# Seven block products for eight in the gate and value layers of the last two token tiles

## The chip, the cores and the metric

The program runs on one core of a Trainium2 chip. The metric is the time of the whole program in device microseconds. Beside the plain runs, one execution was profiled; its trace has a time, a unit and a source line for every instruction. The units are named as in the profile: PE does the matmuls, PEld loads their weights, DVE and ACT work element by element and read PE's results out of PSUM, POOL works element by element in SBUF, and SP issues the DMAs.

## What is computed

An attention with random features is followed by a gated feed-forward layer, all in float32:

```
proj = x @ omega.T                       # q and k, 8 batches, 8 heads, 576 rows, 64 -> 128 features
phi  = exp(proj - |x|^2/2 - max) / sqrt(128)
kv, z = phi(k).T @ v, sum(phi(k))        # per batch and head
attn  = (phi(q) @ kv) / (phi(q) @ z + 1e-6)
X     = attn, heads side by side         # 4608 tokens x 512
g, val = X @ w_gate, X @ w_val           # 512 -> 1536
out   = (silu(g) * val) @ w_out          # 1536 -> 512
```

## The kernel before, in words

**Tiles and operands.** The tokens lie in nine tiles of 512, numbered 0 to 8. The 1536 columns of the hidden layer are twelve blocks `f` of 128, in four sets of three. For the feed-forward layer every float32 operand is held as two parts, `hi` (rounded by ACT) and `lo` (the remainder, subtracted by POOL or DVE), and a product is three matmuls: hi·hi, hi·lo, lo·hi. `x` is kept as `xh`, `xl` in four rotating buffers, weights as `whi`, `wlo`.

**A visit** is one tile with one set of blocks. `stream` issues it: for each of the three blocks a gate product `g` (`mm1`, L633 to L641: four chunks of 128 along 512, three matmuls each, so 12 matmuls of 128x512 into one PSUM bank), SiLU on ACT (L707), then a value product `v` (12 matmuls), the product with the gate on DVE (L721), the hi part of the result `hh` on ACT (L724) and its lo part `hl` on POOL (L725). Four down products `o` of 9 matmuls each follow (`down`, `mm2`, L644 to L650), one for each 128 tokens. They are put into a float32 accumulator `acc`: for the first set by a copy on ACT (L671), after that by an addition on DVE (L674); after the last set the rows are stored (L678). A visit is 3·12 + 3·12 + 4·9 = 108 matmuls. When the next visit uses another set, its weights are loaded into three rotating buffers `wraw` from a scratch array in HBM, rounded by ACT (L242) and subtracted by POOL (L243).

**Rounds.** `ROUNDS` (L60) says which tiles go through the four sets together: 0 to 2, 3 and 4, 5 and 6, 7 and 8.

**Attention** runs in 72 steps of two groups of 256 rows. A step projects on PE (`st_project`, `pp`, L393), takes maxima on DVE, exponentials on ACT (L425), and so on, down to `q_out`, which puts the finished rows into `xh`, `xl` (L626, L627). Attention has four PSUM banks (pools `ps_p`, `ps_a`, `ps_k`) and the SBUF pool `att`; the feed-forward layer has the other four banks (`ps_m`).

**What sets the order.** `course` (L182 to L199) is a plan: for each attention step, how much of the stream of visits shall have been issued by then. It is a string pulled tight between a lower bound (a buffer of `x` must come free) and an upper bound (a tile must be complete), and it ends at the last step at `upper[NN]` (L192). The main loop issues, at six places in a step, as much of the stream as the plan is owed; after the loop whatever is left follows. A scheduler then orders the instructions of each engine; each engine executes its own in order.

Of the kernel before, what the change touches and what calls it, by code (L numbers as in the profile page):

```python
# [23 lines left out]
def kernel(  # L24
# [34 lines left out]

    ROUNDS = [range(0, 3), range(3, 5), range(5, 7), range(7, 9)]  # L60

# [20 lines left out]
    ps_m = ctx.enter_context(tc.tile_pool(name="ps_m", bufs=4, space=PSUM))  # L82
    att = ctx.enter_context(tc.tile_pool(name="att", bufs=2))
    ps_p = ctx.enter_context(tc.tile_pool(name="ps_p", bufs=2, space=PSUM))
    ps_a = ctx.enter_context(tc.tile_pool(name="ps_a", bufs=1, space=PSUM))
    ps_k = ctx.enter_context(tc.tile_pool(name="ps_k", bufs=1, space=PSUM))

# [103 lines left out]
    course = (lower + upper) / 2  # L191
    course[0], course[NN] = 0.0, upper[NN]  # L192
    for _ in range(20000):
# [40 lines left out]

    def new_weights(f, i):
        hi = wpool.tile([P, DM], F32R, name=f"whi{f}_{i}", tag=f"whi{i}")
        lo = wpool.tile([P, DM], F32R, name=f"wlo{f}_{i}", tag=f"wlo{i}")
        weights[f, i] = hi, lo
# [50 lines left out]

    def load_weights(f, i):  # L290
        need(f, i)
        new_weights(f, i)
        raw = moe.tile([P, DM], F32, name=f"wraw{f}_{i}", tag="wraw", bufs=3)
        nc.sync.dma_start(raw, wscr[f, i])
        split_piece(f, i, raw)
# [367 lines left out]
    def down(j, k_, ht, wts, next_set, tt):  # L663
        fs = sorted(ht)
        po = ps_moe(f"o{j}_{k_}_{tt}", [P, DM])
        for n, f in enumerate(fs):
            need(f, 2)
            mm2(po, ht[f], weights[f, 2] if wts is None else wts[f], tt, n == 0, n == FA - 1)
        if k_ == 0:
            acc[j, tt] = accp.tile([P, DM], F32, name=f"acc{j}_{tt}", tag="acc")  # L670
            nc.scalar.copy(acc[j, tt], po)  # L671
        else:
            a_ = acc[j, tt]
            nc.vector.tensor_tensor(a_, po, a_, op=ALU.add)  # L674
        if k_ == NSET - 1:
            a_ = acc.pop((j, tt))
            for o in range(0, P, RES):
                nc.sync.dma_start(rows_of(TILES[j][0] + tt * P + o), a_[o : o + RES, :])  # L678
        if next_set is not None and tt == TILES[j][1] // P - 1:
            for n in range(FA):  # L680
                load_weights(next_set * FA + n, 2)

    def stream():

        todo = []
        for vi, (j, s_, k_) in enumerate(visits):
            nxt = visits[vi + 1] if vi + 1 < len(visits) else None
            new_set = nxt and nxt[1] != s_
            w = TILES[j][1]
            while not avail(j):  # L690
# [18 lines left out]
            if new_set:  # L709
                for f in fs:  # L710
                    load_weights(nxt[1] * FA + f - fs[0], 0)
            while todo:
                down(*todo.pop(0))
                yield MM2
            for f in fs:
# [11 lines left out]
                if new_set:  # L727
                    load_weights(nxt[1] * FA + f - fs[0], 1)
            at_visit[0] = vi + 1
            wts = {f: weights[f, 2] for f in fs} if vi else None  # L730
            todo = [(j, k_, ht, wts, nxt[1] if new_set else None, tt) for tt in range(w // P)]
        for a in todo:
            down(*a)
            yield MM2
# [63 lines left out]
    for n in range(NN):  # L798
# [5 lines left out]
        for what in order:  # L804
            if what is not SHARE:
                what(n)
            if n < EARLY or what is SHARE:
# [5 lines left out]
                left -= 1  # L813
        load_z(n)
    for _ in ma:
        pass
# [30 lines left out]
```

## Time and profile before

| | us |
|---|---|
| median of 3 runs | 1244.59 |
| lowest, highest | 1243.67, 1246.83 |
| the profiled execution | 1241.44 |
| its span, first to last instruction | 1239.3 |
| PE busy in the span | 1206.6 |
| ACT, DVE, POOL busy | 585.3, 520.7, 504.4 |

In the answers of the trace, a group's row gives line, engine, operation, output and inputs by the program's names, shapes, count, then busy time and the mean of one in ns, then the idle time before them and what ended it. A window's row gives, for each engine, busy us and in brackets the instructions, then the granted clock of PE as a share of full speed, the busy share of the DMA engines and GB/s. A row of the chain of work that ended last gives start, length, engine, tile, line, count.

### The profile page before, as it was taken

Reading aid. Unit: us, or ns where it says so; the run is one execution under the profiler, and the core shown is the slowest. Engines: PE = TensorE matmul, PEld = TensorE weight load, DVE = VectorE, ACT = ScalarE, POOL = GpSimd, SP = SyncE. Lnnn points to the kernel's source line nnn. Section 1 sums busy time; section 2 is a strip of 40 time slices with the busy share of each in tenths; the row PEclk is TensorE's granted clock in tenths of the full one; section 3 lists DMA queues with packets and bytes.
Section 4 is the critical chain, followed back from the end, with each engine's and each line's share of the span. In section 5 each row is a group of like instructions: output and inputs, shape, how many; then the busy total and the mean of one; then the engine's idle time right before and its main releaser. Section 6 shows DMA issues by size and latency. Waiting matters only on the chain. (4 is left out here: it accounts for less than half of the span.)

```text
span 1239.3 us, 18373 instructions
## 1 busy us (share of the span) xinstructions
PE 1206.6 (97%) x6849; PEld 991.8 (80%) x6849; DVE 520.7 (42%) x1068; ACT 585.3 (47%) x1310; POOL 504.4 (41%) x436
## 2 busy tenths in 40 slices
PE   6999998999999999999999999989999999999998
PEld 5888787788888888877888878867887877788886
DVE  4887867435556424443334444332233322002212
ACT  3878775543445334455654465434634422332220
POOL 3333334354534322335554453335645421333431
PEclk7999999999999999999999999999999999999999
DMA  5555545324334322222222222212201021111202
GB/s 147 140 139 150 147 139 149 109 76 136 108 94 139 85 62 54 63 71 77 69 60 71 58 64 60 52 35 61 69 26 51 27 60 34 51 51 30 61 13 69
DMA packets 157689, 97.76 MB, mean 79 GB/s; under 512 B 119680, under 2 KB 132000, under 8 KB 157600
## 3 DMA queue, kind: packets, MB, share of 16 engines
q1 hardware_dynamic: 157600, 96.59, 29.3%
q8 instruction: 54, 0.88, 0.3%
q14 instruction: 35, 0.29, 0.1%
HBM read 77.66 MB, written 18.89 MB: 78 GB/s over the span
## 5 line engine op out<-in xcount | busy, mean ns | idle before, releaser
L243 POOL TENSOR_TENSOR wlo<-wraw,whi 128x512 fp32r<-128x512 f32 x108 | 139.1, 1298 | 157.9 <-ACT whi L242 157.7
L725 POOL TENSOR_TENSOR hl<-sl,hh 128x512 fp32r<-128x512 f32 x108 | 140.3, 1302 | 121.3 <-ACT hh L724 121.2
L650 PE MATMUL o<-whi,hh 128*128 128x512 f32 x432 | 172.9, 401 | 2.0 <-ACT hh L724 2.0
L425 ACT ACTIVATE ph<-pp,st 128x128 f32<-128x128 f32 x576 | 158.6, 382 | 32.8 <-DVE st L414 32.3
L650 PE MATMUL o<-whi,hl 128*128 128x512 f32 x432 | 169.6, 393 | 2.6 <-POOL hl L725 2.5
L641 PE MATMUL v<-xh,whi 128*128 128x512 f32 x432 | 172.0, 398 | 0.0
L641 PE MATMUL g<-xh,whi 128*128 128x512 f32 x432 | 171.0, 397 | 0.5 <-ACT xh L626 0.5
L641 PE MATMUL g<-xl,whi 128*128 128x512 f32 x432 | 169.0, 392 | 0.5 <-DVE xl L627 0.5
L650 PE MATMUL o<-wlo,hh 128*128 128x512 f32 x432 | 169.0, 391 | 0.0
L641 PE MATMUL v<-xl,whi 128*128 128x512 f32 x432 | 168.9, 391 | 0.0
L641 PE MATMUL v<-xh,wlo 128*128 128x512 f32 x432 | 168.8, 391 | 0.0
L641 PE MATMUL g<-xh,wlo 128*128 128x512 f32 x432 | 168.7, 391 | 0.0
L377 POOL TENSOR_TENSOR sq<-nat 128x512 f32<-128x512 f32 x72 | 76.6, 1065 | 186.7 <-DMA nat<-in_k_dram 135.4
L724 ACT CAST hh<-sl 128x512 fp32r<-128x512 f32 x108 | 67.1, 625 | 173.1 <-DVE sl L721 173.0
L674 DVE TENSOR_TENSOR acc<-o,acc 128x512 f32<-128x512 f32 x108 | 74.0, 688 | 170.6 <-PE o L650 170.4
L721 DVE TENSOR_TENSOR sl<-v,sl 128x512 f32<-128x512 f32 x108 | 74.0, 688 | 159.0 <-PE v L641 156.7
L242 ACT CAST whi<-wraw 128x512 fp32r<-128x512 f32 x108 | 66.8, 623 | 148.0 <-PE v L641 81.4
L411 DVE TENSOR_REDUCE st<-pp 128x4 f32<-128x512 f32 x144 | 93.5, 684 | 80.2 <-PE pp L393 79.9
L393 PE MATMUL pp<-omT,x 64*128 64x128 f32 x1152 | 97.8, 295 | 2.8 <-DVE xl L627 1.4
L393 PEld LDWEIGHTS pp<-omT,x 64*128 64x128 f32 x1152 | 80.7, 195 | 23.2 <-issue 14.6
L650 PEld LDWEIGHTS o<-whi,hh 128*128 128x128 f32 x432 | 81.6, 189 | 21.8 <-ACT hh L724 3.1
L650 PEld LDWEIGHTS o<-whi,hl 128*128 128x128 f32 x432 | 81.4, 189 | 21.7 <-POOL hl L725 4.3
(67 smaller groups left out, 1815.7 us busy)
## 6 DMA issues: line engine op xcount, KB each, us to landing
wraw<-wscr SPq DMA_DIRECT2D x108, 256.0 KB, 2.7
wscr<-wc SPq DMA_DIRECT2D x36, 256.0 KB, 2.3
out_dram<-acc SPq DMA_DIRECT2D x72, 128.0 KB, 2.4
nat<-in_k_dram SPq DMA_DIRECT2D x64, 128.0 KB, 3.1
v<-in_v_dram SPq DMA_DIRECT2D x64, 128.0 KB, 3.2
nat<-in_q_dram SPq DMA_DIRECT2D x64, 128.0 KB, 2.6
st<-in_moe_w_gate_dram SPq DMA_DIRECT2D x12, 512.0 KB, 5.3
st<-in_moe_w_val_dram SPq DMA_DIRECT2D x12, 512.0 KB, 4.1
```

What stands on the lines that cost most here:

```text
L242: nc.scalar.copy(hi, raw)
L243: nc.gpsimd.tensor_tensor(lo, raw, hi.bitcast(F32), op=ALU.subtract)
L377: nc.gpsimd.tensor_tensor(sq, nat, nat, op=ALU.mult)
L393: nc.tensor.matmul(pp[hh][:, i, c, :], x[r, i, c * P : (c + 1) * P], omT[r], start=True, stop=True)
L411: nc.vector.tensor_reduce(st[:, 1, :, :, hh], pp[hh], axis=AX.X, op=ALU.max, negate=True)
L425: nc.scalar.activation(ph[:, c, hh * M : (hh + 1) * M], pp[hh][:, i, c, :], AF.Exp, bias=st[:, 3, i, c, hh : hh + 1], scale=1.0,)
L641: nc.tensor.matmul(ps, a_[:, ws], b_[:, c, :], start=n == 0, stop=n == 3 * NC - 1)
L650: nc.tensor.matmul(ps, a_[:, ts_], b_, start=first and n == 0, stop=last and n == 2)
L674: nc.vector.tensor_tensor(a_, po, a_, op=ALU.add)
L721: nc.vector.tensor_tensor(h, pv, h, op=ALU.mult)
L724: nc.scalar.copy(hh, h)
L725: nc.gpsimd.tensor_tensor(hl, h, hh.bitcast(F32), op=ALU.subtract)
```

## The change

The last two tiles, 7 and 8, leave the rounds. Their gate and value products are done at the end, together, in six pairs of blocks (`pf` 0 to 5; each has a gate half, `i` = 0, and a value half, `i` = 1). For a pair, the weights are a 2x2 array of parts (two halves of the 512 inputs, two blocks), and `x` is another (two halves, two tiles). The four results are formed by seven products of parts, in Winograd's form, in place of eight: `a11·b11`, `a12·b21`, `s4·b22`, `a22·t4`, `s1·t1`, `s2·t2`, `s3·t3`, where the `s` are sums and differences of weight parts and the `t` of `x` parts. A product is two chunks by three matmuls, 6 matmuls of 128x512. Three PSUM banks `a`, `c`, `d` take the seven products of a half: `a` takes products 1, 6, 7, 4 on top of each other, `c` takes 5 and 3, `d` takes 2. What a bank holds in between is copied out by ACT (`m1`, `m5`, `u2`) and added on DVE (`plus`).

Around that:

- `load_seven` loads the two raw gate (or value) blocks of a pair, forms `s1` to `s4` on DVE (four operations of 128x256), rounds on ACT and subtracts on POOL. `make_t` forms the four `t` for all of `x`, two chunks with 8 DVE operations, 4 ACT roundings and 4 DVE subtractions of 128x512 each.
- Down products take two blocks (6 matmuls) for each 128 tokens, and the accumulator of tiles 7 and 8 gets six parts in place of four. The four `down` of tile 8 and then the four of tile 7 stand between the products of the next pair.
- When the attention loop is over, the pool `att` and the four PSUM banks of attention are closed, and the pools `win` (SBUF) and `ps_w` (four banks) take their place.
- The plan ends 25 us of stream (`MARGIN`) short of the end of its rounds.

The diff, cut to its core:

```
-    ROUNDS = [range(0, 3), range(3, 5), range(5, 7), range(7, 9)]
+    ROUNDS = [range(0, 3), range(3, 5), range(5, 7)]
+    LASTA, LASTB = 7, 8
+    NPF = NF // 2
+    MARGIN = 25.0
...
-    course[0], course[NN] = 0.0, upper[NN]
+    course[0], course[NN] = 0.0, upper[NN] - MARGIN
...
+    def load_seven(pf, i):
+        win = late_pools["win"]
+        raws_ = []
+        for f in (2 * pf, 2 * pf + 1):
+            raw = moe.tile([P, DM], F32, name=f"wraw{f}_{i}s", tag="wraw", bufs=3)
+            nc.sync.dma_start(raw, wscr[f, i])
+            raws_.append(raw)
+        (a11, a12), (a21, a22) = ((r[:, 0:G], r[:, G:DM]) for r in raws_)
+        s = win.tile([P, 4, G], F32, name=f"s{pf}_{i}", tag="s")
+        s1, s2, s3, s4 = (s[:, n] for n in range(4))
+        nc.vector.tensor_tensor(s1, a21, a22, op=ALU.add)
+        nc.vector.tensor_tensor(s3, a11, a21, op=ALU.subtract)
+        nc.vector.tensor_tensor(s2, s1, a11, op=ALU.subtract)
+        nc.vector.tensor_tensor(s4, a12, s2, op=ALU.subtract)
...
+            nc.scalar.copy(hi, src_)
+            nc.gpsimd.tensor_tensor(lo, src_, hi.bitcast(F32), op=ALU.subtract)
...
+    PROD = {1: ("a11", "b11"), 2: ("a12", "b21"), 3: ("s4", "b22"), 4: ("a22", "t4"), 5: ("s1", "t1"), 6: ("s2", "t2"), 7: ("s3", "t3")}
+    def product(ps, n, wts, start):
+        (wh, wl), (xh, xl) = wts[PROD[n][0]], ts[PROD[n][1]]
+        for c in range(CH):
+            w_ = slice(c * P, (c + 1) * P)
+            for m, (a_, b_) in enumerate(((wh, xh), (wh, xl), (wl, xh))):
+                nc.tensor.matmul(
+                    ps, a_[:, w_], b_[:, c, :],
+                    start=start and c == 0 and m == 0, stop=c == CH - 1 and m == 2, skip_group_check=True,
+                )
...
+            def gate(n, src_):
+                nc.scalar.activation(sl[n], src_, AF.Silu)
+            def value(n, src_):
+                nc.vector.tensor_tensor(sl[n], src_, sl[n], op=ALU.mult)
+                nc.scalar.copy(hh[:, n], sl[n])
+                nc.gpsimd.tensor_tensor(hl[:, n], sl[n], hh[:, n].bitcast(F32), op=ALU.subtract)
...
+                a, c, d = (ps_w.tile([P, T], F32, name=f"{e}{pf}_{i}", tag="w") for e in "acd")
+                product(a, 1, wts, True)
+                copy("m1", a)
+                product(c, 5, wts, True)
+                copy("m5", c)
+                if one_down():
+                    yield MM2
+                product(a, 6, wts, False)
+                copy("u2", a)
+                product(c, 3, wts, False)
+                plus(1, c, "u2")
+                if one_down():
+                    yield MM2
+                product(a, 7, wts, False)
+                plus(3, a, "m5")
+                product(d, 2, wts, True)
+                plus(0, d, "m1")
+                if one_down():
+                    yield MM2
+                product(a, 4, wts, False)
+                use(2, a)
+                if pf + 1 < NPF:
+                    load_seven(pf + 1, i)
+                if one_down():
+                    yield MM2
...
+    late.close()
...
+    late_pools["mt"] = make_t()
+    for _ in late_pools["mt"]:
+        give(1.0)
```

How the change moves instructions is shown at three places. **The first** is PE where attention step 67 begins (`g` and `v` are gate and value products of a visit, `pp` the projection of attention, `ptq` transposes). Before, the end of a value product and the next visit's gate:

```order
L641 MATMUL v_2_8496<-xh_6752,whi_1_7332 128x512
L641 MATMUL v_2_8496<-xl_6753,whi_1_7332 128x512
L641 MATMUL v_2_8496<-xh_6752,wlo_1_7333 128x512
L641 MATMUL g_3_8520<-xh_6028,whi_0_8430 128x512
L641 MATMUL g_3_8520<-xl_6029,whi_0_8430 128x512
L641 MATMUL g_3_8520<-xh_6028,wlo_0_8431 128x512
```

The same place now:

```order
L647 MATMUL v_2_8496<-xh_6752,whi_1_7332 128x512
L647 MATMUL v_2_8496<-xl_6753,whi_1_7332 128x512
L647 MATMUL v_2_8496<-xh_6752,wlo_1_7333 128x512
L399 MATMUL pp_67_8512<-omT,x_8373 128x128
L399 MATMUL pp_67_8513<-omT,x_8373 128x128
```

Up to this place PE's instructions are the same, one by one, in both programs (3588 of them). From here on a step has fewer matmuls of the stream: before, each of the steps 66 to 70 has 108 of them up to the next step's projection, now 72, 63, 69, 60 and 60. Behind the last attention matmul there were 756 and are now 999.

**The second** is ACT at the end of the first pair: `m_1` and `u_1` are copies out of the banks `c` and `a` of its value half, `whi_1_…` roundings of the next pair's value weights, `whi_2_…` of its down weights, `hh0s` the hi part of the result, `m_0` the first copy of the next pair. Before, ACT at the last change of a set of weights:

```order
L707 ACTIVATE sl_0_11035<-g_0_10996 128x512
L707 ACTIVATE sl_1_11037<-g_1_11009 128x512
L707 ACTIVATE sl_2_11039<-g_2_11022 128x512
L242 CAST whi_2_11085<-wraw_2_11087 128x512
L242 CAST whi_2_11091<-wraw_2_11093 128x512
L242 CAST whi_2_11097<-wraw_2_11099 128x512
L724 CAST hh_0_11117<-sl_0_11035 128x512
```

Now:

```order
L873 COPY u_1_10266<-a_1_10241 128x512
L248 CAST whi_2_10335<-wraw_2_10337 128x512
L783 CAST whi_1_1_10323<-s_1_10314 128x512
L861 CAST hh0s<-sl_1_10091 128x512
L248 CAST whi_2_10341<-wraw_2_10343 128x512
L783 CAST whi_1_2_10327<-s_1_10314 128x512
L861 CAST hh0s<-sl_3_10093 128x512
L783 CAST whi_1_3_10331<-wraw_1s 128x256
L861 CAST hh0s<-sl_0_10090 128x512
L861 CAST hh0s<-sl_2_10092 128x512
L873 COPY m_0_10362<-a_0_10353 128x512
```

Roundings that wait for a load now stand ahead of copies that PE waits for. **The third** is POOL at the same place, where it makes the lo parts. Before:

```order
L243 TENSOR_TENSOR wlo_2_10746<-wraw_2_10747,whi_2_10745 128x512
L243 TENSOR_TENSOR wlo_2_10752<-wraw_2_10753,whi_2_10751 128x512
L243 TENSOR_TENSOR wlo_2_10758<-wraw_2_10759,whi_2_10757 128x512
L725 TENSOR_TENSOR hl_3_10778<-sl_3_10695,hh_3_10777 128x512
L725 TENSOR_TENSOR hl_4_10796<-sl_4_10697,hh_4_10795 128x512
L725 TENSOR_TENSOR hl_5_10814<-sl_5_10699,hh_5_10813 128x512
```

Now:

```order
L784 TENSOR_TENSOR wlo_1_0_10320<-wraw_1s,whi_1_0_10319 128x512
L249 TENSOR_TENSOR wlo_2_10336<-wraw_2_10337,whi_2_10335 128x512
L784 TENSOR_TENSOR wlo_1_1_10324<-s_1_10314,whi_1_1_10323 128x512
L862 TENSOR_TENSOR hl0s<-sl_1_10091,hh0s 128x512
L249 TENSOR_TENSOR wlo_2_10342<-wraw_2_10343,whi_2_10341 128x512
L784 TENSOR_TENSOR wlo_1_2_10328<-s_1_10314,whi_1_2_10327 128x512
L862 TENSOR_TENSOR hl0s<-sl_3_10093,hh0s 128x512
```

The lo parts of the result (`hl0s`) stand among those of the next weights, where before they stood behind them.

More of the change, by code (lines that the diff above doesn't have):

```diff
@@ L233, with new_weights @@
     converted = set()
-    def new_weights(f, i):
-        hi = wpool.tile([P, DM], F32R, name=f"whi{f}_{i}", tag=f"whi{i}")
-        lo = wpool.tile([P, DM], F32R, name=f"wlo{f}_{i}", tag=f"wlo{i}")
+    def new_weights(f, i, pool=None):
+        hi, lo = (
+            (pool or wpool).tile([P, DM], F32R, name=f"w{e}{f}_{i}", tag=f"w{e}{i}") for e in ("hi", "lo")
+        )
         weights[f, i] = hi, lo
@@ L814 @@
         load_z(n)
+    late.close()
+    for name, pool in (
+        ("win", tc.tile_pool(name="win", bufs=1)),
+        ("ps_w", tc.tile_pool(name="ps_w", bufs=4, space=PSUM)),
+    ):
+        late_pools[name] = ctx.enter_context(pool)
+    late_pools["mt"] = make_t()
+    for _ in late_pools["mt"]:
+        give(1.0)
     for _ in ma:
```

124 lines of the change are left out of this document (111 added, 13 removed).

## The prediction, on record before the change was run

> **What bounds the kernel now.** I read the totals first, then windows, then the chain of waits from the end, then what PE waited for.
>
> ```profile
> span 1239.3 us, 18373 instructions
> PE 1206.6 (97%) x6849; PEld 991.8 (80%) x6849; DVE 520.7 (42%) x1068; ACT 585.3 (47%) x1310; POOL 504.4 (41%) x436
> ```
>
> PE is the only engine near the span. A share of 97% is an average, so the windows have to say where it holds:
>
> ```profile
> 620.00:744.00 124.00, 123.98 (x734) 99.53 (x732) 51.86 (x106) 68.37 (x149) 63.31 (x55) 1.00 0.24 64
> 868.00:992.00 124.00, 124.00 (x627) 99.92 (x626) 38.65 (x83) 58.87 (x117) 66.22 (x58) 1.00 0.16 43
> 1085.00:1116.00 31.00, 31.00 (x138) 25.70 (x137) 3.44 (x5) 9.93 (x17) 11.50 (x9) 1.00 0.17 51
> 1178.00:1209.00 31.00, 31.00 (x139) 25.66 (x138) 4.84 (x7) 6.72 (x11) 9.20 (x8) 1.00 0.03 9
> ```
>
> From 620 us on PE has no hole, in attention and in the pure feed-forward stage, at a granted clock of 1.00. In the last stage ACT and POOL are busy for 10 and 12 of 31 us, DVE for 3. The chain that ended last says what the last stage is made of:
>
> ```profile
> 1060.44 1.07 PE xt L607 x20
> 1061.51 0.02 issue
> 1061.53 0.38 ACT xh L626
> ...
> 1061.96 8.46 PE g L641 x36
> ...
> 1192.81 8.16 PE v L641 x36
> 1200.97 8.16 PE g L641 x36
> 1209.13 8.16 PE o L650 x36
> 1217.29 5.45 PE v L641 x24
> ...
> 1228.31 6.44 PE o L650 x27
> 1234.75 0.02 issue
> 1234.77 0.69 DVE acc L674
> ```
>
> Attention ends on PE at 1061.5 (`xt`). From there to 1234.75 it is matmul after matmul of 128x512, in blocks of 36 that take 8.16 us whether they are `g`, `v` or `o`: **0.2267 us for a matmul**. This is the price I use, not the 391 to 401 ns of the page's group rows, which overlap. After the last one come 0.69 us of DVE and the stores, up to the span's end at 1239.3. What PE waits for in the part that the change touches is small:
>
> ```profile
> PE o L650 <- POOL hl L725: 1.2, 2, 0.6
> PE g L641 <- ACT xh L626: 0.5, 1, 0.5
> ```
>
> (window from 868 us to the end). So the stage is bound by the number of matmuls, and nothing else is near.
>
> **Up to step 67 nothing changes.** PE's order is the same for the first 3588 instructions. Where that ends in time:
>
> ```profile
> L393 PE MATMUL pp<-omT,x x80: 272/272/373, 864.2 to 978.9; 64*128 64x128 f32 x80
> ```
>
> (from 740 us on, 16 records for a step: steps 67 to 71.) Step 67's projection starts at 864.2, and 36 matmuls (8.2 us) earlier, at 856, the programs part.
>
> **Do the lighter steps get shorter?** After 856 the attention steps carry 60 to 72 matmuls of the stream in place of 108. The step's length can be read on both sides of that:
>
> ```profile
> 607.30 1.29 DVE L411 TENSOR_REDUCE st<-pp 128x4 f32<-128x512 f32 x2 [0.52 <-PE pp L393]
> 741.32 1.29 DVE L411 TENSOR_REDUCE st<-pp 128x4 f32<-128x512 f32 x2
> 865.42 1.29 DVE L411 TENSOR_REDUCE st<-pp 128x4 f32<-128x512 f32 x2 [8.48 <-PE pp L393]
> 979.16 1.29 DVE L411 TENSOR_REDUCE st<-pp 128x4 f32<-128x512 f32 x2 [8.55 <-PE pp L393]
> ```
>
> The first two are nine steps apart: 134.0/9 = 14.9 us a step, which carries about 48 matmuls, 10.9 us; attention itself takes 4.0. The last two are four steps apart: 28.4 us a step with 108 matmuls, 24.5; attention takes 3.9. The sum holds at 48 and at 108, so I take it at 63 too: 14.3 + 4 = 18.3 us. Between the last attention matmul and the end there are then 999 matmuls and not 756, but what counts is the total. Attention should end 315 matmuls, 71 us, sooner, at 990 us.
>
> **The sum, part by part.**
>
> *Removed matmuls.* A half of a pair needs 7·6 = 42 matmuls in place of 4·12 = 48; twelve halves save 72. The down products stay at 288 (8 by 6 by six pairs; before 8 by 9 by four sets). 72 · 0.2267 = **−16.3 us**. The new matmuls have the same 128x512 shape, so the price holds.
>
> *Work added to the other engines.* Prices, from the stage after 1050 us (ACT, POOL, DVE), and loads and stores:
>
> ```profile
> L242 ACT CAST whi<-wraw 128x512 fp32r<-128x512 f32 x27 | 16.9, 624 | 54.9 <-PE v L641 27.6 <-PE g L641 14.6 <-PE o L650 12.3
> L707 ACT ACTIVATE sl<-g 128x512 f32<-128x512 f32 x21 | 12.5, 594 | 22.4 <-PE g L641 21.1 <-POOL hl L725 1.4
> L671 ACT COPY acc<-o 128x512 f32<-128x512 f32 x8 | 4.7, 587 | 10.4 <-PE o L650 10.4
> L725 POOL TENSOR_TENSOR hl<-sl,hh 128x512 fp32r<-128x512 f32 x23 | 29.6, 1287 | 37.0 <-ACT hh L724 37.0
> L674 DVE TENSOR_TENSOR acc<-o,acc 128x512 f32<-128x512 f32 x24 | 16.6, 692 | 73.9 <-PE o L650 73.9
> L627 DVE TENSOR_TENSOR xl<-xt,xh 128x256 fp32r<-128x256 f32 x2 | 0.8, 424 | 9.6 <-ACT xh L626 9.5
> wraw<-wscr SPq DMA_DIRECT2D x108, 256.0 KB, 2.7
> out_dram<-acc SPq DMA_DIRECT2D x72, 128.0 KB, 2.4
> ```
>
> A pair is 132 matmuls, 29.9 us. In it ACT has 6 copies, 4 SiLU, 12 full and 2 half roundings, about 14.1 us. POOL has 12 full and 2 half subtractions, 12 · 1.29 + 1.4 = 16.9. DVE has 18 full operations and 8 of 256 columns (nearest row 0.42): 12.4 + 3.4 = 15.8. None comes above 60%, so in total all of it lies beside PE: **0**. What could still cost is order, at three places.
>
> *The `t`.* 16 DVE operations and 8 subtractions, 24 · 0.69 = 16.6 us, and 8 roundings. They start when the last `xh`, `xl` are there; product 5, the first that reads a `t`, comes 171 + 6 matmuls later, 40.1 us. DVE has 13 operations of the visits and 8 for the `s` beside them, 12.4 us. 29 of 40: hidden; without that cover it would cost what is over. Closing attention's pools costs nothing: the loads and matmuls that wait for these banks and buffers have theirs free by then.
>
> *Bank hand-overs in the steady pairs.* Products 6, 3 and 7 accumulate on a bank that ACT has to copy out first. Between the product before and the one that waits stand 12 other matmuls, 2.72 us, against a copy of 0.59. It is tightest at the change of pairs, because ACT's order puts two roundings of down weights ahead of the first copy. With the last product 4 ending at 0, PE does a down product to 1.4, product 1 to 2.7, product 5 to 4.1, a down product to 5.4 and then wants `m1` copied. ACT's first rounding must wait for the last reader of its buffer, the down product, at 1.4; then rounding 2.0, `hh` 2.7, accumulator copy 3.3, rounding 3.9, `m1` 4.6. That is **0.8 us early**: 0. If this cover were gone, six pair changes at a fraction of a us each is what it costs; behind the copy wait product 6 on PE and everything after.
>
> *The first pair* has no down products of its own between its products, so all intervals are short. Set 0 at the end of product 7 of its value half. Product 2, product 4, and the next pair's products 1 and 5 follow to 5.4; then the first down product, whose sixth matmul (at 6.6) reads the lo part of block 3. POOL's order puts six full subtractions up to and with that one. They start with a down weight whose load had to wait for a buffer: product 4 of the gate half ends at −5.2, a half rounding and a half subtraction free the buffer at −4, load 2.7, rounding 0.6, so POOL starts at −0.6 and is done at −0.6 + 6 · 1.29 + gaps = 7.2 to 7.6. **PE waits 0.6 to 1; I take +1.0.** Bounds: 0 if the load lands a little sooner; +4 if it takes twice as long and the queue shifts with it.
>
> *The ends.* Now PE waits 0.6 for `hl` in the last visit and some 0.7 around 1061.5 for `xh` (36 matmuls in 8.46, not 8.16, behind 0.38 of ACT). After the change the last eight down products begin with tile 8, whose parts come from products 3 and 7, done 4 us before; and the last attention matmul is followed by down products that don't read it. **−1.2**, bounds −1.5 and 0. The stores get closer: 256 KB every 6 · 0.2267 = 1.36 us in place of 2.04.
>
> ```profile
> 1232.00:1234.00 2.00, 2.00 (x11) 1.65 (x10) 0.69 (x1) 0.00 (x0) 0.00 (x0) 1.00 0.57 131
> 994.00:996.00 2.00, 2.00 (x13) 1.42 (x10) 0.52 (x3) 2.00 (x6) 2.00 (x3) 1.00 0.72 210
> ```
>
> They move 131 GB/s now at 57% of the DMA engines and would need 193; 210 was reached. **+0.3**, bounds 0 and +2.
>
> Sum: −16.3 + 1.0 − 1.2 + 0.3 = **−16.2 us**. From the profiled execution's 1241.44 (2.1 over its span) that gives 1225.2. The median of the runs shown is 3.15 above the profiled execution; moved by the same amount, 1244.59 − 16.2 = **1228.4; I say 1228**. A measurement of this kernel can tell 0.3%, 3.7 us.
>
> *DVE beside POOL.* The `s`, the `t` and value times gate read SBUF alone and are new in this stage beside POOL's subtractions. Rows of such operations in before (ns: min, median, max):
>
> ```profile
> L262 DVE TENSOR_SCALAR wc<-wc x36: 412/426/1534, 18.3 to 400.9; 128x512 f32<-128x512 f32 x36
> L266 DVE SCALAR_TENSOR_TENSOR st<-st,wc x36: 676/692/1684, 19.2 to 402.3; 128x512 int32<-128x512 int32 x36
> ```
>
> The longest is longer than the median by 1.0 to 1.1 us, close to one POOL operation of 1.29, but the medians are the undisturbed times. If in every pair the 8 `s` (0.42 each) and 4 multiplications (0.69), 6.1 us, held POOL up for all their length, POOL would need 16.9 + 6.1 = 23.0 of 29.9 us: still hidden. Only at the first pair, where POOL is late already, would a collision reach PE; I price it at 0, at most +1.1 each. The Trainium skill ("SBUF — State Buffer", section "Who interferes with whom") says that a VectorE instruction with two SBUF inputs and a GpSimd instruction that reads SBUF share a port, one blocking the other for its whole length. The long maxima agree with it, the medians say that it is rarely met; by the rule at the first pair the sum would be about 1 us more, 1229.
>
> **The rivals.**
>
> *A, slower: the copies come late in every half.* ACT executes in order, and every half has at least one copy that PE waits for (`m1`, `m5`, `u2`) behind a rounding that waits for a raw load. The ring of three raw buffers turns once in load 2.7 + rounding 0.62 + subtraction 1.29 = 4.6 us. The cover of a copy is 2.72 − 0.59 = 2.1 us. If each of the twelve halves met one whole turn at its worst, PE would lose 12 · (4.6 − 2.1) = 30 us: **1258**. It comes out slower than before by 0.3% once 20 us are lost (16.2 + 3.7), 1.65 us a half, that is when copies come 3.7 us later than their matmuls allow at no loss. For it speaks that loads wait for this ring already:
>
> ```profile
> SPq L294 <- POOL wlo L243: 238.1, 45, 23.8
> ```
>
> (868 us to the end: SP waited 45 times for POOL to give a buffer back.) Against it: those waits are SP's, 238 us of them, so a load stands ready as soon as a buffer is free, and in my walk of the change of pairs, where the queue is worst, the copy is still 0.8 us early; ACT is busy for 14.1 of 29.9 us and catches up between. The Trainium skill ("Perfetto Trace Analysis", section "Optimizing Tensor Performance", "Matmuls") asks that independent matmul groups rotate through different PSUM banks, so that the emptying of one overlaps the next. Here three of seven products go back to a bank just used; were nothing between, 36 such copies at 0.59 would cost 21 us, 1250; the order shows 12 other matmuls between, so I don't take it. Chance of A 0.08.
>
> *B, part of the gain lost in small waits.* My walk has a margin of 0.8 us from rows that themselves spread by a few tenths, at a dozen half changes; if each costs 0.65 us, the margin gone and half as much again, or the first pair meets its bound of +4 and a few of them the rest, 7.8 us go: **1236**. For it: three engines hand over within 3 us at every half, and a late `hl` has no second tile to cover it. Against it: 0.2 to 0.6 us is all that before shows of such waits in 370 us. Chance 0.16.
>
> *C, no change: the steps don't shorten, or the end stalls.* The order fixes the count of matmuls, so the change can only fail to do what it says if something else sets the pace. Were the five lighter steps held at, say, 21 us by attention's own chain, PE would idle 2.7 us in each, 13.5 us: **1242**. The steps of 14.9 us with 48 matmuls speak against it directly. Chance 0.06.
>
> **How the numbers follow.** The forecast, 1228, has 0.70. Its own range: with the good ends of the three uncertain terms (0, −1.5, 0) the sum is −17.8, with the bad ones (+4, 0, +2) it is −10.3, so 1226.8 to 1234.3 on the median; the 3.15 between profile and median may shrink with another set of runs, which takes the low end to 1225, and the runs before reach 2.2 above their median, which takes the high end to 1237. This holds B's 1236 too and leaves out A, C and a little of both sides: **1225 to 1237**. Faster by over 0.3% (below 1240.9) are the forecast and B, 0.86; within it C, 0.06; slower A, 0.08.
>
> **What would show it.** Right: PE has 72 matmul records fewer; attention's last matmul ends near 990 us; steps after 856 are near 18.3 us; in the last 200 us PE has no hole beyond one of about 1 us for `hl` at the first down products of the first pair (near 1062 us: 720 matmuls before the end); the chain's end is matmuls at 0.2267 each; ACT, DVE and POOL stay under 60% there; the span is near 1223. Wrong: PE's waits name ACT's `m`, `u` copies with more than 5 us together (A or B), the last `xt` is not 65 to 75 us earlier (C), or a matmul of a late product takes longer than 0.2267 though nothing is waited for, which no row of before excludes for banks that are written on top of each other by separate groups.

## The result, and the profile after

| | before | after |
|---|---|---|
| median of 16 runs, us | 1243.46 | 1231.76 |
| lowest, highest | 1238.65, 1249.95 | 1225.84, 1244.70 |
| profiled execution | 1241.44 | 1232.11 |
| its span | 1239.3 | 1229.9 |

The ratio is 0.990, with a 95% interval of 0.9881 to 0.9919: faster, by 10 to 15 us. The time lies within the range of the prediction (1225 to 1237), 3.8 us above the predicted 1228; between the medians lie 11.7 us, where 16.2 were forecast. One of the 16 runs after the change, the 1244.70, had a lower granted clock than the others (0.978) and is left out of the ratio. The profiled execution has two stretches that have to be kept apart. First the totals of the page, then the projections of steps 67 to 71 after the change, 16 records a step:

```profile
PE 1193.3 (97%) x6777; PEld 978.9 (80%) x6777; DVE 607.8 (49%) x1192; ACT 624.6 (51%) x1387; POOL 549.3 (45%) x469
```

```profile
L399 PE MATMUL pp<-omT,x x80: 272/272/373, 859.5 to 933.8; 64*128 64x128 f32 x80
```

PE has 6777 records in place of 6849, 72 fewer. The projection of step 67 starts at 859.5. Up to it PE's instructions are those of before, and there they ended at 856: this execution was 3.5 us late before it came to the change. So I compare only what lies behind, from this projection to the start of the last accumulator addition, and call it **the late stretch**. Before, its beginning is at 856.07 us: the last matmul that both programs share starts at 855.75 there, and after the change the projection starts 0.32 us behind that matmul. In that kernel the stretch is 1234.77 − 856.07 = 378.7 us. After, the end is

```profile
1212.87 12.25 PE o L656 x54
1225.12 0.02 issue
1225.14 0.69 DVE acc L680
```

(the end of the chain of waits), 1225.14 − 859.54 = 365.6: **13.1 us less**. PE's waits behind 850 us are four, and they say where the rest of the gain went:

```profile
PE o L656 <- ACT sl L714: 1.7, 1, 1.7
PE o L656 <- POOL hl0s L862: 0.9, 1, 0.9
PE v L647 <- DVE acc L680: 0.7, 1, 0.7
PE a L832 <- DVE c L877: 0.3, 1, 0.3
```

Only the one for `hl0s` had been counted on. Behind each wait the matmuls need some 0.1 to 0.2 us to be back at their pace; counted as what lies between the starts of matmuls beyond 0.2267 us each, the four cost 1.82, 1.04, 0.88 and 0.50 us, and all losses from the last `xt` to the last matmul come to 5.7 us. Behind 1068.7 us there is none:

```profile
1100.00:1130.00 30.00, 30.00 (x134) 24.82 (x134) 15.65 (x26) 13.44 (x25) 18.22 (x15) 1.00 0.21 57
```

(a window in the steady pairs, columns as before: PE full, DVE, ACT and POOL at 52, 45 and 61%.)

**Where the waits come from.** They stand in two places, around 1022 to 1027 us, while the `t` are made, and in the first pair, 1061 to 1068. The timeline of DVE shortly before the first one (start, length, engine, line, operation, output and inputs, in brackets the idle time ahead and who ended it):

```profile
1017.19 0.68 DVE L817 TENSOR_TENSOR t3f<-t3f,t0f 128x512 f32<-128x512 f32 x1
1017.79 1.78 DVE L817 TENSOR_TENSOR t4f<-xh,t2f 128x512 f32<-128x512 f32 x1
1019.50 1.77 DVE L822 TENSOR_TENSOR t1l<-t2f,t1h 128x512 fp32r<-128x512 f32 x1
1021.19 0.68 DVE L817 TENSOR_TENSOR t4f<-t4f,xl 128x512 f32<-128x512 f32 x1
```

and of POOL at the same time:

```profile
1017.30 1.72 POOL L784 TENSOR_TENSOR wlo<-wraw_0s,whi 128x512 fp32r<-128x512 f32 x1 [0.58 <-ACT whi L783]
1019.13 1.59 POOL L784 TENSOR_TENSOR wlo<-s,whi 128x512 fp32r<-128x512 f32 x1
```

The same operation of the same size takes 0.68 us or 1.78, and POOL's take 1.59 and 1.72 in place of 1.29, where the two overlap. What ACT did then:

```profile
1021.90 0.62 ACT L821 CAST t3h<-t4f 128x512 fp32r<-128x512 f32 x1 [2.36 <-DVE t4f L817]
1022.43 0.61 ACT L783 CAST whi<-s 128x512 fp32r<-128x512 f32 x1
1022.95 0.59 ACT L714 ACTIVATE sl<-g 128x512 f32<-128x512 f32 x1
```

and PE:

```profile
1023.59 0.50 PE L656 MATMUL o<-whi,hh 128*128 128x512 f32 x1 [1.66 <-ACT sl L714]
```

ACT waits 2.36 us for the late `t4f`. Behind that rounding, in the same queue, stands the SiLU of a visit that has nothing to do with the `t`, and the bank that this SiLU empties is wanted by PE for a down product. The second wait hangs on the same `t4f`: the rounding of `s`, then POOL's subtraction, then the `s` of the value half that wait for it on DVE, and behind these the additions to the accumulators. So no `t` is late for its own product; what stands **behind** the `t` in two in-order queues is.

### The profile page after: what moved, and what is told of

It reads as the page before. It is cut to its first block, busy times and chain, and to the rows that moved or that the text cites. A ratio compares the mean times of both kernels' runs of the same rounds, so it can differ in the third digit from the quotient of the medians.

```text
span 1229.9 us, 18546 instructions
## 1 busy us (share of the span) xinstructions
PE 1193.3 (97%) x6777; PEld 978.9 (80%) x6777; DVE 607.8 (49%) x1192; ACT 624.6 (51%) x1387; POOL 549.3 (45%) x469
## 5 line engine op out<-in xcount | busy, mean ns | idle before, releaser
L656 PE MATMUL o<-whi,hh 128*128 128x512 f32 x336 | 135.5, 403 | 3.8 <-ACT hh L733 2.0
L647 PE MATMUL v<-xh,whi 128*128 128x512 f32 x336 | 134.5, 400 | 0.7 <-DVE acc L680 0.7
L656 PE MATMUL o<-whi,hl 128*128 128x512 f32 x336 | 132.3, 394 | 2.3 <-POOL hl L734 2.3
L647 PE MATMUL g<-xl,whi 128*128 128x512 f32 x336 | 131.7, 393 | 0.5 <-DVE xl L633 0.5
L656 PE MATMUL o<-wlo,hh 128*128 128x512 f32 x336 | 131.6, 392 | 0.0
L647 PE MATMUL v<-xh,wlo 128*128 128x512 f32 x336 | 131.4, 391 | 0.0
L647 PE MATMUL g<-xh,wlo 128*128 128x512 f32 x336 | 131.3, 392 | 0.0
L647 PE MATMUL v<-xl,whi 128*128 128x512 f32 x336 | 131.2, 391 | 0.0
L410 DVE TENSOR_REDUCE st<-sq 128x8 f32<-128x512 f32 x72 | 49.1, 682 | 105.0 <-POOL sq L383 105.0
L494 POOL TENSOR_TENSOR jk<-ph,zt 128x512 f32<-128x512 f32 x32 | 41.1, 1290 | 103.6 <-ACT ph L431 86.8
```

What stands on the lines that cost most here:

```text
L647: nc.tensor.matmul(ps, a_[:, ws], b_[:, c, :], start=n == 0, stop=n == 3 * NC - 1)
L656: nc.tensor.matmul(ps, a_[:, ts_], b_, start=first and n == 0, stop=last and n == 2)
```

## The experiments

The theory after the first look: DVE operations with both inputs in SBUF and POOL's subtractions shut each other out. The main rival: the order alone, in which other work stands behind the `t`, makes the waits at any speed of the `t`. In the table, the late stretch is read as above; "lost" is the sum of PE's losses from the last `xt` to the last matmul, of the profiled execution.

| run | median us (runs) | ratio to before, 95% | late stretch | lost |
|---|---|---|---|---|
| before | 1243.5 (16) | 1 | 378.7 | 1.7 |
| the change | 1231.8 (16) | 0.9900 (0.9881 to 0.9919) | 365.6 | 5.7 |
| e1 POOL quieter | 1226.4 (4) | 0.9881 (0.9840 to 0.9922) | 362.4 | 2.5 |
| e2 lo of `t` on POOL | 1236.2 (5) | 0.9938 (0.9905 to 0.9971) | 370.8 | 10.9 |
| e3 `hl0s` on DVE | 1232.7 (4) | 0.9913 (0.9878 to 0.9947) | 365.7 | 5.8 |
| e4 eight products | 1243.3 (10) | 1.0005 (0.9977 to 1.0032) | 378.4 | 2.2 |
| e5 `t` in PSUM | 1228.0 (6) | 0.9871 (0.9845 to 0.9898) | 362.3 | 2.4 |
| e6 `hl0s`, `m1` on DVE | 1232.0 (4) | 0.9894 (0.9856 to 0.9932) | 365.8 | 5.9 |
| e7 `t`, `c` in PSUM, `hl0s`, `m1` on DVE | 1226.0 (5) | 0.9848 (0.9823 to 0.9874) | 360.5 | 0.6 |
| e9 `t` and `c` in PSUM | 1225.6 (4) | 0.9870 (0.9833 to 0.9907) | 361.5 | 1.6 |
| e10 e7 without `m1` | 1229.7 (4) | 0.9877 (0.9840 to 0.9914) | 360.5 | 0.6 |

Medians of 4 to 6 runs scatter by some us; differences below that are read from the late stretch and from what PE loses in it. How well these repeat, a second profile of the same work shows (e8, below, is the change with a piece added at the very end): 133.3 us to the last `xt` and 5.7 us lost, both as in the change.

**e1: the lo parts that POOL makes in that stretch become copies on ACT.**

```
+    def low(lo, src_, hi):
+        if quiet[0]:
+            nc.scalar.copy(lo, src_)
+        else:
+            nc.gpsimd.tensor_tensor(lo, src_, hi.bitcast(F32), op=ALU.subtract)
...
-        nc.gpsimd.tensor_tensor(lo, raw, hi.bitcast(F32), op=ALU.subtract)
+        low(lo, raw, hi)
...
```

(`quiet[0]` is set when the attention loop is over and taken back before the first pair; the other two places that call `low` are cut.)

> From the end of attention to the first pair the lo parts that POOL makes (weights, results of the last visits, parts for the first pair) are replaced by ACT copies of the same size, so these lo parts hold the wrong numbers; DVE's work is the same. Theory (DVE operations with both inputs in SBUF and POOL's subtractions shut each other out): the operations of make_t take 0.68 to 0.70 us each, none 1.7; PE's two waits during make_t (1.66 us behind `sl`/`acc` and 0.72 behind `acc`) are gone; the two waits in the first pair (0.34 behind `c`, 0.89 behind `hl`) stay; about 3 us faster than the change, 1229. Rival (the order alone: the accumulator additions stand behind the t operations on DVE, which would be late at any speed of theirs): the two waits stay at 1.5 us or more together, 1232.

What PE waits for from 860 us on is now

```profile
PE o L664 <- POOL hl0s L871: 0.9, 1, 0.9
PE a L840 <- DVE c L886: 0.4, 1, 0.4
```

Both waits around the `t` are gone, the other two stay, the late stretch is 3.2 us shorter. That is the theory's side. Its "none 1.7" was wrong: six subtractions stay on POOL in this stretch, three of weights and three of a visit's results that the program issues ahead of the end of attention. They make the run a measure of the dose. The `t` operations' busy time (all 16 sums, then all 8 lo parts), in the change and in e1:

```profile
980.00:1060.00 80.00, 14.96 (x16) 1.00 0.26 69
980.00:1060.00 80.00, 9.80 (x8) 1.00 0.26 69
```

```profile
980.00:1060.00 80.00, 13.32 (x16) 1.00 0.26 70
980.00:1060.00 80.00, 7.61 (x8) 1.00 0.26 70
```

24.8 and 20.9 us. In the 34 us behind the last `xt` (windows, columns as before) POOL runs 11 operations in the change and 6 in e1:

```profile
992.80:1026.80 34.00, 31.62 (x138) 25.23 (x137) 32.38 (x42) 12.40 (x23) 16.44 (x11) 1.00 0.16 41
```

```profile
999.00:1033.00 34.00, 34.00 (x150) 28.14 (x151) 31.01 (x45) 15.12 (x30) 10.24 (x6) 1.00 0.25 66
```

**e5: the sums lie in the PSUM banks that are free there; POOL's and PE's order are those of the change.** (DVE's and ACT's differ from it in a few places around the `t`.)

```
-            b12, t1, t2, t3, t4 = (
-                win.tile([P, T], F32, name=f"t{n}f{c}", tag="sl", bufs=5) for n in range(5)
+            b12, t1, t2, t3 = (
+                ps_w.tile([P, T], F32, name=f"t{n}f{c}", tag="w") for n in range(4)
             )
+            t4, b22 = b12, win.tile([P, T], F32, name=f"b22f{c}", tag="sl", bufs=5)
...
```

> The sums of make_t (b12 and the full t1 to t4) lie in the four PSUM banks that are free until the first pair, in place of SBUF; nothing is left out, and the order of PE and POOL is the same as in the change. Of the 24 DVE operations 4 still have both inputs in SBUF (b12 and b22 of each half), the other 20 have one in PSUM. Theory (what shuts DVE and POOL out is that both inputs come from SBUF): the 20 take 0.68 to 0.70 us beside the same POOL work, at most the other 4 take 1.7; the two waits during make_t (1.66 + 0.72 us) are gone, 2.7 us less from the last xt to the last matmul than in the change (231.9 us there), 1228.5 to 1229.5. Rival (POOL's activity slows any operation of DVE, or the waits come from the order): operations of 1.2 us and more among the 20, waits of 1.5 us and more together, 1232.

```profile
980.00:1060.00 80.00, 11.04 (x16) 1.00 0.28 73
980.00:1060.00 80.00, 5.19 (x8) 1.00 0.28 73
```

Now 16.2 us, with POOL at its work as before: 0.67 to 0.70 each, only one `b12` (`t0f<-xh,xl`, both inputs in SBUF) takes 1.13 and lifts the mean of its row:

```profile
L818 DVE TENSOR_TENSOR t0f<-xh,xl 128x512 f32<-128x512 f32 x2 | 1.8, 915 | 0.0
L823 DVE TENSOR_TENSOR t1l<-t2f,t1h 128x512 fp32r<-128x512 f32 x2 | 1.4, 678 | 0.0
```

Against these 16.2 us the change pays 8.5 us for 11 POOL operations and e1 4.7 us for 6: **0.78 us of DVE's time for each** on average, in both. PE's waits from 860 us on are

```profile
PE o L656 <- POOL hl0s L863: 0.9, 1, 0.9
PE a L833 <- DVE c L878: 0.4, 1, 0.4
```

Both waits around the `t` are gone (3.3 us in the late stretch; expected 2.7), and the median, 1228.0, is half a us below what the theory had. So it was neither the order nor POOL's being busy, but the place of the second input.

**e8: the same by itself**, in 12 DVE additions behind the program's end (one run, whose time can't be compared; `A`, `B`, `X`, `Y` are in SBUF, `Q` in PSUM, `ND` is 12):

```
+    def stage(first, pool, two):
+        for n in range(ND):
+            nc.vector.tensor_tensor(O, first, B, op=ALU.add)
+            if pool and n % 2 == 0:
+                nc.gpsimd.tensor_tensor(Z, X, Y, op=ALU.subtract)
...
+    stage(A, False, 0)
+    stage(A, True, 0)
+    stage(Q, False, 0)
+    stage(Q, True, 0)
```

> The change, and behind its work a piece that the reference doesn't have: DVE additions of 128x512 float32 (12 in each part) with both inputs in SBUF, alone and then beside 6 POOL subtractions, and with one input in PSUM, alone and then beside 6 POOL subtractions. Theory: 0.69 us alone both ways; beside POOL the additions with both inputs in SBUF wait for whole POOL operations, 1.7 us and more for some, or POOL's take up to 1.75, and the two together take about the sum of both; with one input in PSUM 0.69 each and POOL 1.29 each. Rival: the same durations with PSUM as with SBUF.

```profile
1237.27 14.33 DVE L1025 TENSOR_TENSOR prb<-prb,prb 128x512 f32<-128x512 f32 x12 [2.82 <-ACT prp L1035]
1253.84 8.67 DVE L1025 TENSOR_TENSOR prb<-prq,prb 128x512 f32<-128x512 f32 x12 [2.24 <-ACT prp L1031]
1265.60 8.67 DVE L1025 TENSOR_TENSOR prb<-prq,prb 128x512 f32<-128x512 f32 x12 [3.10 <-ACT prp L1035]
```

```profile
1237.38 10.04 POOL L1027 TENSOR_TENSOR prp<-prp,prp 128x512 f32<-128x512 f32 x6 [14.78 <-ACT prp L1035]
1265.71 7.98 POOL L1027 TENSOR_TENSOR prp<-prp,prp 128x512 f32<-128x512 f32 x6 [18.29 <-ACT prp L1035]
```

Beside six POOL subtractions, 12 additions out of SBUF take 14.33 us; with one input in PSUM (`prq`) 8.67, as much as with POOL idle (second row). Of POOL's six, 10.04 us against 7.98. What the two lose together is 5.66 + 2.06 = 7.7 us, 1.29 for each POOL operation: as much as one whole subtraction, shared between them. The additions alone from SBUF ran in part among other work, at 0.68 each. The Trainium skill ("SBUF — State Buffer", section "Who interferes with whom") says just this: a VectorE instruction with two SBUF inputs contends with a GpSimd instruction that reads SBUF; one with at most one such input, outside VectorE's 2-port modes, does not. By the sum of the losses the trace agrees. The longest addition takes 1.63 us and the longest subtraction 1.70, so no single operation was seen to wait for the whole length of another, as the prediction had put it.

**e2: the eight lo parts of the `t` go to POOL.**

```
-                nc.vector.tensor_tensor(lo, full, hi.bitcast(F32), op=ALU.subtract)
+                nc.gpsimd.tensor_tensor(lo, full, hi.bitcast(F32), op=ALU.subtract)
```

> The 8 lo subtractions of make_t go from DVE to POOL; nothing is left out. Theory: DVE has 16 operations in place of 24 in this stretch (11.0 us at 0.69, and with one collision for each POOL operation at most 8 us more), POOL 10.3 us more; the two waits during make_t together fall from 2.4 us to under 0.8; 1 to 3 us faster than the change, 1229 to 1231. Rival (any SBUF work on POOL is paid on DVE in full): as many collisions as before plus 8, the waits stay, 1232 or more.

Slower than the change, as the rival said (1236.2, 1232 or more expected), but by a wait that it had not named. DVE is lighter, but now POOL's queue is late for the results of the last visits:

```profile
PE o L656 <- POOL hl L734: 3.6, 1, 3.6
```

Most of its subtractions take 1.72 to 1.75 us next to the 16 sums, and an `hl` of the last visit but one stands behind seven of the eight new ones. Two more waits, 0.8 and 0.6 us, stand a little earlier, and behind the long one eleven matmuls in a row take 0.427 us each in place of 0.227. The granted clock (third column from the end) is at half there:

```profile
1024.00:1028.80 4.80, 4.80 (x13) 3.74 (x12) 0.47 (x2) 0.00 (x0) 4.30 (x4) 0.50 0.23 55
```

So this wait cost over 2 us more than its own length; behind the change's wait of 1.66 us the clock is 1.00. Work moved off the overfull engine onto the one that it collides with is paid twice.

**e3 and e6: the first pair.** e3 makes its four `hl0s` on DVE; e6 moves the copy `m1` of the second pair to DVE as well.

```
-                nc.gpsimd.tensor_tensor(hl[:, n], sl[n], hh[:, n].bitcast(F32), op=ALU.subtract)
+                (nc.gpsimd if pf else nc.vector).tensor_tensor(hl[:, n], sl[n], hh[:, n].bitcast(F32), op=ALU.subtract)
```

> The four lo parts of the first pair's results (`hl0s`) are made by DVE in place of POOL; nothing is left out. Theory (they are late because POOL has five other subtractions ahead of them, some of them slowed to 1.75 us): PE's wait of 0.89 us for `hl0s` is gone, the other three waits stay; 1 us faster, 1231. Rival (what is late is the input `sl`, through DVE's own slowed operations): the wait stays at 0.5 us or more and moves to DVE.

```
-                    nc.scalar.copy(keep[name], ps)
+                    if name == "m1" and pf == 1 and i == 0:
+                        nc.vector.tensor_copy(keep[name], ps)
+                    else:
+                        nc.scalar.copy(keep[name], ps)
```

> As in the run before with the first pair's `hl0s` on DVE, and the copy `m1` of the second pair's gate half on DVE too, in place of ACT; nothing is left out. Theory (two queues are late at the same place, POOL with `hl0s` and ACT with `m1` behind roundings that wait for loads; each hides the other): the wait of 0.89 to 1.04 us is gone, the three others stay, 1.1 us less than the change from the last xt to the last matmul. Rival (a third queue is as late): a wait of 0.5 us or more remains within 5 us of that place.

Nothing is won: the wait moves by one queue each time.

```profile
PE a L832 <- ACT m L873: 1.0, 1, 1.0
```

```profile
PE a L832 <- DVE m L874: 1.1, 1, 1.1
```

(e3, then e6.) In e3 the wait for `hl0s` goes, as the theory had it, but one of the same length takes its place; in e6 the rival is right, a third queue is as late. It is DVE's:

```profile
1061.40 1.61 DVE L860 TENSOR_TENSOR sl<-c,sl 128x512 f32<-128x512 f32 x1
1064.63 1.78 DVE L862 TENSOR_TENSOR hl0s<-sl,hh0s 128x512 fp32r<-128x512 f32 x1
1068.04 1.22 DVE L860 TENSOR_TENSOR sl<-c,sl 128x512 f32<-128x512 f32 x1
```

Three of the four products of value and gate (those with `c`) have both inputs in SBUF, too, and so do the new `hl0s`. In e3 the copy waits on ACT behind the rounding of the last of these products.

**e9, e7, e10: the same cure there.** In e9 `c` of products 3 and 2 stays in its bank (beside the `t` of e5), so two of the three products with `c` have an input in PSUM; e7 has `hl0s` and `m1` on DVE too; e10 is e7 with `m1` back on ACT.

```
-                    o = sl[n] if i == 0 else moe.tile([P, T], F32, name=f"c{pf}_{n}", tag="hl", bufs=FA)
+                    if i == 0:
+                        o = sl[n]
+                    elif n == 3:
+                        o = moe.tile([P, T], F32, name=f"c{pf}_{n}", tag="hl", bufs=FA)
+                    else:
+                        o = ps
```

> The sums of make_t in PSUM and the value sums c of products 3 and 2 kept in their banks; `hl0s` stays on POOL and all copies on ACT; nothing is left out. Theory (the wait for `hl0s` is POOL's three subtractions of 1.6 to 1.75 us in place of 1.29, held up by DVE's products of value and gate, and the wait for `c` is such a product of 1.57 us): the wait of 0.34 us behind `c` is gone, that for `hl0s` falls from 0.89 to 0 to 0.5; the time that PE loses from the last xt to the last matmul is under 1.3 us (2.4 with the sums of make_t in PSUM alone). Rival (the wait for `hl0s` is POOL's order alone): it stays at 0.9.

> The sums of make_t in PSUM, the value sums c of products 3 and 2 kept in their banks (so that the product with the gate has one input in PSUM), `hl0s` and the second pair's `m1` on DVE; nothing is left out. Theory: the four waits of the change (1.66, 0.72, 0.34, 0.89 us) are all gone; 226.5 us of matmuls from the last xt to the last matmul and under 1.5 us beside, against 231.9 in the change; 4 to 5 us faster than the change, 1227 to 1228. Rival: the order that the scheduler makes anew brings waits of its own, 1229 to 1232.

> As the kernel with all three edits, but the second pair's copy `m1` is on ACT again; nothing is left out. Theory (with DVE's products no longer slowed, ACT's roundings of `hh0s` ahead of `m1` come early enough): PE waits less than 0.5 us for `m`, under 1.1 us lost in all from the last xt to the last matmul, the time within 1.5 us of the kernel with all three edits (1226). Rival (the copy is late behind ACT's roundings whatever DVE does): a wait of 0.8 us or more for `m`.

In e9 the wait for `c` is gone, but that for `hl0s` falls only to 0.8:

```profile
PE o L656 <- POOL hl0s L863: 0.8, 1, 0.8
```

Of the six POOL operations up to the one that PE waits for, one still takes 1.75, the others 1.28 to 1.30. So the collision can make at most 0.5 us of this wait; the rest is POOL's order, nearer the rival's side. In e7 all four waits are gone; the late stretch is 5.1 us shorter than in the change, and from the last `xt` to the last matmul PE loses 0.6 us of 227:

```profile
L399 PE MATMUL pp<-omT,x x80: 272/272/373, 856.3 to 930.5; 64*128 64x128 f32 x80
L680 DVE TENSOR_TENSOR acc<-o,acc x9: 691/692/692, 1205.8 to 1216.7; 128x512 f32<-128x512 f32 x9
```

(the start of the late stretch, and its end as the last of the additions.) e10 shows that `m1` needn't move: its late stretch is the same, with no wait for `m`. Its median is 3.7 us above e7's on 4 runs, more than was expected; in the profiled executions step 67 starts at 863.6 and at 856.3, so the difference lies ahead of the late stretch there. e7, at 1226.0 and 0.9848 of before, is faster than both kernels. The medians don't tell e5, e7, e9 and e10 apart; by the late stretch, `t` and `c` in PSUM and `hl0s` on DVE are what shortens it.

**e4: the seven products undone.** Tiles 7 and 8 keep their pairs, banks, plan and down products, with two full products for each result:

```
+                for n, (k, o) in enumerate(((0, 0), (0, 1), (1, 0), (1, 1))):
+                    ps = ps_w.tile([P, T], F32, name=f"a{pf}_{i}_{n}", tag="w")
+                    mm1(ps, weights[2 * pf + k, i], xt[LASTB if o else LASTA])
+                    use(2 * k + o, ps)
...
```

> The seven products are undone: tiles 7 and 8 are done in the same six pairs, with the same banks, the same MARGIN and the same down products, but with eight plain products of 12 matmuls a half pair (two for each result, accumulated in its bank), no s, no t, no copies. Theory (the gain is the 72 matmuls and nothing else; the rest of the structure is worth nothing, the new DVE work costs 3 to 4 us): 1231.8 + 16.3 - 4 = 1244, like before within 2 us; PE without a hole over 0.5 us from 860 us on. Rival (pairing, the plan that ends early or the buffers cost something themselves, and the seven products are worth their full 16.3 us with no loss): 1248 or more.

1243.3, as before within 0.3 us, the late stretch 378.4 against 378.7. So all that the change wins is the 72 matmuls, and the pairs, the plan that ends early and the buffers are worth nothing that can be measured. Its two waits are for lo parts by POOL (`hl0s` 1.1, `hl5s` 0.4 us), none while the `t` would be made. "Without a hole over 0.5 us" was wrong by that first one, which stands in this kernel too, though its products have one input in PSUM and POOL's operations take 1.25 to 1.30 us each: one more sign that POOL's order makes it.

## Why the prediction was right, and where it was off

- **What bounds it** (PE's count of matmuls): right. Where nothing is lost, a matmul takes 0.2267 us, and undoing the seven products gives the 16.3 us back up to the losses (e4's late stretch is 12.8 us longer than the change's, and it loses 3.5 us less).
- **Lighter steps**: right. The four steps from 67 to 71 take (933.8 − 0.9 − 859.5)/4 = 18.3 us each, as forecast; the last `xt` comes 133.3 us behind the start of the late stretch, before it was 205.4: 72.1 us earlier, 71.4 were forecast (315 matmuls); a wait for `hl` of 0.6 us ahead of the last `xt` is gone, too.
- **First pair, +1.0**: right in place and size, the size in part by luck. `hl0s` cost 0.89 us of waiting, 1.04 with the restart. In e9 the six POOL operations take 8.0 us and PE waits 0.8, as in my walk (7.8 to 8.2, and 0.6 to 1). But in the change itself three of the six are slowed (1.61, 1.75, 1.74) and they take 8.9, while PE comes 0.5 us later, held up by `c`: neither was in the walk. That two more queues were as late behind it, I had not seen.
- **Room beside PE in the steady pairs**: right; DVE 52, ACT 45, POOL 61% busy, POOL a little over the 60 named.
- **Bank hand-overs**: right. In the change and in e7 no copy of `m` or `u` makes PE wait; rival A found no place. In e3 and e6 such a copy is waited for once, because of DVE.
- **The ends, −1.2 and +0.3**: right, the first a little small. The waits at the last `xt` and in the last visit, which with their restarts make up nearly all of before's 1.7 us of losses, are gone; from the last addition to the end of the span it is 4.8 us, before 4.5.
- **The `t`, hidden: wrong.** This is the step that failed: "29 of 40: hidden". It was sized at 0.69 us an operation and held against the time of product 5 alone. Measured, the 24 `t` operations take 24.8 us, not 16.6 (0.78 more for each of POOL's 11 operations), and what had a nearer due time than product 5 were the SiLU and the additions of the last visit behind them. Cost: 1.82 + 0.88 = 2.7 us with the restarts, 3.3 us in the late stretch (e5), which holds some gaps of 0.1 to 0.2 us beside them.
- **DVE beside POOL**: the rows were read the wrong way. I took the medians of L262 and L266 (0.43, 0.69) for the price and the maxima (1.53, 1.68) for a rare mishap. But the medians are those of operations that mostly had no POOL operation beside them: in the trace of before 23 of the 36 of L262 had none and took 0.41 to 0.43 us, and of the 13 that met one, 11 took 0.79 to 1.53. L262 has only one input, so two inputs in SBUF are not the only case that collides. And these rows come from the first 400 us. How often the two meet has to be read from the stretch in question, and around the `t` POOL is busy for 16.4 of 34 us, with subtractions out of SBUF. I also let POOL pay for it, where DVE pays 0.94 of 1.29 us (e8: 5.66 and 2.06 us over six). With 0.78 for each of 11 subtractions the sum in the prediction would have read 16.6 + 8.6 + 12.4 = 37.6 of 40.1 us, a full queue, and the question what stands behind it would have come up. The rule of the Trainium skill ("SBUF — State Buffer", section "Who interferes with whom") stood beside it and was applied to the first pair alone. The wait for `c` (0.34 us, 0.50 with the restart) is the same thing in the first pair.

Together: 16.5 us were forecast for the late stretch (without the stores). The `t` took 3.3 of them, `c` 0.5, and the last `xt` came 0.7 us earlier than forecast: 13.4, against 13.1 measured. Of the 0.3 us between them I can say only that the ends gave 0.5 more than forecast, and that 0.6 us of gaps of about 0.1, which e7 shows as well, go against it. As to the chances, the gain came with a part lost in waits, which was to be B: B's mechanism (many small waits at the half changes) didn't occur, the forecast's with one term mis-sized did.

## What to carry to other kernels

Before element-wise work is called hidden on an engine with time to spare, look where its inputs lie and what the neighbour does: here an operation of DVE with both inputs in SBUF paid 0.78 us for each subtraction that POOL ran beside it, and keeping one of the inputs in PSUM, where four banks were free, took the price away. (An operation with one input can pay as well: L262 in before did.) And check an added piece of work not against its own due time alone, but against that of everything that stands behind it in the queues it goes through; moving it to the queue of the engine that it collides with made it worse.

## What the runs showed of the hardware that I had not expected

- The collision takes time from both sides. In e8 the sum was as much as all of POOL's own work, 7.7 us over six operations of 1.29; DVE's work there was nearly as long (8.67), so the run doesn't tell whether POOL's length or DVE's sets it.
- Behind PE's wait of 3.6 us in e2 the granted clock was 0.50 for 4.8 us, and a matmul took 0.427 us; behind the wait of 1.66 us in the change it was 1.00.
- PE's first instructions, the same one by one up to step 67, took from 856.1 us (before) and 856.3 (e7) to 865.7 (e1). In e1 the granted clock of the first 50 us was 0.66, in the change 0.83 (the clock is the third column from the end):

```profile
0.00:50.00 50.00, 39.03 (x229) 35.55 (x229) 23.27 (x44) 21.68 (x64) 17.69 (x33) 0.66 0.54 128
```

```profile
0.00:50.00 50.00, 39.21 (x317) 35.54 (x319) 29.17 (x62) 28.50 (x86) 19.04 (x34) 0.83 0.60 147
```

  229 matmuls in place of 317 were done by then. Other late starts (864.2 in e9) have 0.83 there, and e6, with 1.00, starts at 861.5, so the clock of the first 50 us is not all of it. Either way, nearly 10 us of scatter arise before the place of a change of 12 us, and a stretch cut out of the trace tells such edits apart where four runs don't.
